# A retention layer with an ELU feed-forward: one early load asked for later, and an opening planned with other piece times

## The chip, the cores and the metric

The kernel runs on one core of one Trainium2 chip. The metric is the device time of one execution in microseconds, over several runs. The core has a matrix engine (TensorE, PE in the profile, with a separate path PEld that loads weights), a vector engine (VectorE, DVE), an engine for activations and copies (ScalarE, ACT), a general engine (GpSimd, POOL) and an engine that only issues transfers (SyncE, SP). Each engine works through its own list of instructions in order; between engines they wait on semaphores. Transfers can be asked for by SP, ACT and POOL; 16 DMA engines carry them out.

## What is computed

Retention over 8 batches, 8 heads, 576 positions and 64 values per head, then a feed-forward with 512 inputs, 2048 hidden values and an ELU:

```python
scores = scale * np.matmul(q, k.transpose(0, 1, 3, 2))
gamma = 1.0 - 2.0 ** (-5.0 - np.arange(H, dtype=np.float32))
Dmat = np.where(rel >= 0, gamma[:, None, None] ** rel[None, :, :], 0.0)
attn = np.matmul(scores * Dmat[None], v)             # q, k, v: (8, 8, 576, 64)
x = attn.transpose(0, 2, 1, 3).reshape(B * S, H * D)     # (4608, 512)
h = x @ w_in                                             # w_in: (512, 2048)
g = np.where(h > 0.0, h, np.exp(np.minimum(h, 0.0)) - 1.0)
out = g @ w_out                                          # w_out: (2048, 512)
```

## The kernel before

The 512 first positions of each batch are cut into 4 items (2 stretches of 256 positions, called T, by 2 groups of 4 heads, called w); the 64 last positions of all batches make two more items, the tails. An item n goes through these named steps:

- **ldq, ldk, ldv**: its 256 KB pieces of q, k and v are loaded by SP (L375). One of them, v of item 0, is loaded by ScalarE instead; the table `AWAY` (L203) names it and the earliest time at which the planner may place it.
- **cq, ck**: q and k times their decay factors (tiles gq, gk), in two halves each (`scaled`, L445); cq10 is half 1 of q of item 0. **cv**: v cast to bf16 (`cast_v`, L479). They run on DVE, POOL or ACT.
- **T, cp**: four transposes on PE and the copy of their result into tile qkT (`turn_pe`, L491 and L497); T(1,0) is q of item 1, T(1,1) its k.
- **sc, mask**: the products of q and k into tile sc, and their masking on DVE into tile pt (L731).
- **st, mid, end, bm, be**: the running state. st multiplies k by v on PE; mid and end add it up (L678, L680, L687), bm and be spread it into the tiles s_mid and s_end (L709, L695).
- **iv, xc**: on PE, state times queries plus pt times values (`do_inter`, `do_values`); the result is copied into tile xt (L766) by ACT or DVE.

The feed-forward then works on blocks. The first blocks have 256 positions, later ones 512. **F1** (`ffn1`) is 8 matmuls with w_in for a narrow block; **ex** is the exponential on ACT (L878), **md** either a relu (ACT L888 or DVE L890) or, later, an addition on DVE (L892), **g** the last step of the ELU on DVE (L900, L902). **F2** (`ffn2`) multiplies by w_out. The weights come in eight pieces **wi0..3** and **wo0..3**, asked for by POOL (L424, L432). Items 0 to 3, that is batch 0, feed blocks 0 and 1 (F1_0_p and F1_1_p).

The order of the steps on each engine is not written out. Every step is an `Op` with a cost in microseconds for each engine that may run it, the steps it depends on and a rank. `Plan.run` (L66) plays these through: when an engine is free it takes the ready step with the lowest rank; a step with several engines goes to the one that would end it first. Between a step's end and the start of a step on another engine the planner counts `HOP` (L19). The weight pieces have earliest times in `FROM` (L200). The program is then emitted in the planned order, and the chip keeps that order on every engine, but not the planned times. Where the plan leaves PE without work in the first 50 us, matmuls on a tile of zeros are put in its place.

A step `hold4` (L384) on POOL keeps SP's load of q of item 4, and so all of SP's later loads, back until POOL comes to it. The decay factors are three exponentials on ACT (L973 to L975, step `factors`). The completion of the transfers that SP and ACT ask for is counted on eight semaphores that the framework hands out in turn: a ninth transfer waits, before it is issued, until the first one on the same semaphore has landed.

Of the kernel before, what the change touches and what calls it, by code (L numbers as in the profile page):

```python
# [11 lines left out]
FP32 = mybir.dt.float32  # L12
BF16 = mybir.dt.bfloat16
I32 = mybir.dt.int32
AF = mybir.ActivationFunctionType
ALU = mybir.AluOpType

P = 128
HOP = {"PE": 0.22, "DVE": 0.08, "ACT": 0.08, "POOL": 0.1}  # L19
LANES = 6  # L20


class Op:


    def __init__(self, name, cost, deps, emit, rank, take=(), use=(), banks=(), dma=None, after=None):
        self.name, self.cost, self.emit, self.rank = name, cost, emit, rank
        self.deps = [d for d in deps if d is not None]
        self.turn = [] if after is None else [after]
        self.take, self.use, self.banks, self.dma = take, [*use, *(t[1] for t in take)], banks, dma  # L30
        self.eng = self.start = self.end = self.done = None
        self.slot, self.waits, self.at = {}, [], 0.0


class Plan:
# [6 lines left out]
    def add(self, *a, **kw):  # L42
        op = Op(*a, **kw)
        self.ops.append(op)
        for key in op.use:
            self.users.setdefault(key, []).append(op)
            op.turn += self.owner.get(key, [])
        for cls, key, *_ in op.take:
            self.owner[key] = [op]
            if cls not in FREE:  # L50
                op.turn += self.takers.get(cls, [])
                self.takers[cls] = [op]
        return op
# [12 lines left out]
    def run(self, began):  # L66

        self.left = {key: len(u) for key, u in self.users.items()}
        self.freed = {}
        bank, lanes = {}, {"SP": 0, "POOL": 0, "ACT": 0}  # L70
        wire = {"SP": [], "POOL": [], "ACT": []}
        free, order, events = dict(began), [], []
# [51 lines left out]
        while len(order) < len(self.ops) or any(wire.values()) or events:  # L124
            again = True
            while again:
                again = False
                for e in began:
                    if free[e] > now + 1e-9:
                        continue  # L130
                    best = pick(e, now)
                    if best is None:
                        continue
                    _, op, got = best
                    for o in op.cost:
                        ready[o].remove(op)
                    cost = op.cost[e]
                    op.eng, op.start, op.end = e, now, now + (cost[0] if isinstance(cost, tuple) else cost)
                    op.done = None
                    op.waits = [*op.deps, *(bank[b] for b in op.banks if b in bank and bank[b].eng != e)]  # L140
                    for b in op.banks:
                        bank[b] = op
                    op.slot = {}
                    for key, (cls, n) in got.items():
                        if self.slots[cls][n] is not None:
                            op.waits += self.users[self.slots[cls][n]]
                        self.slots[cls][n], op.slot[key] = key, n
# [40 lines left out]

LEAD = 64
HOLD = {4: "wi0"}  # L190
RANKS = {}
TOGETHER = 1
EARLY = 5
LOOSE = True
# [27 lines left out]
def kernel(  # L222
# [140 lines left out]
    def load_main(it, srcs="qkv"):  # L363
# [3 lines left out]
        for s in srcs:  # L367
# [14 lines left out]
            if s == "q" and n in HOLD:  # L382
                def emit_hold(op, key=key):
                    pin(nc.gpsimd.memset(tiles[key][:, 0, 0, :1], 0.0))  # L384

                held.append(add(f"hold{n}", {"POOL": 0.1}, [], emit_hold, -5, take=take))
# [33 lines left out]
    def load_w_in(n0, n1, after):  # L420
        c = slice(n0 * 512, n1 * 512)

        def emit(op):
            pin(nc.gpsimd.dma_start(w_in_sb[:, :, c], moe_w_in[:, c].rearrange("(j p) n -> p j n", p=P)))  # L424

        op = add(f"wi{n0}", {"POOL": 0.8}, [], emit, -1000, dma=(2.75 * (n1 - n0), 32 * (n1 - n0), 4.9), after=after)
        for n in range(n0, n1):
            w_in_ld[n] = op

    def load_w_out(n, after):  # L430
        def emit(op):
            pin(nc.gpsimd.dma_start(w_out_sb[:, 4 * n : 4 * n + 4],  # L432
                                    moe_w_out[n * 512 : (n + 1) * 512, :].rearrange("(f p) n -> p f n", p=P)))

        w_out_ld[n] = add(f"wo{n}", {"POOL": 0.8}, [], emit, -1000, dma=(2.75, 32, 4.9), after=after)

# [47 lines left out]
    def turn_pe(it, i, deps, src, key, dst_cls, n_of, cost):  # L484
# [3 lines left out]
        def emit(op):  # L488
            p = tiles["T", n_of]
            for j in range(4):  # L490
                pin(nc.tensor.transpose(p[:, j], src()[:, j * P : (j + 1) * P], ident))  # L491

        t = add(f"T{n_of}", {"PE": 0.35}, deps, emit, it.rank - 4,
                take=[T("f", ("T", n_of), [P, 4, P], BF16)])

        def emit2(op):
# [332 lines left out]

    def early(it):  # L830
        n = it.n
        sc = add(f"sc{n}", {"PE": 0.4}, it.turned, lambda op: do_scores(it), it.rank,
                 take=[T("sc", ("sc", n), [P, 2, 512], FP32)], use=[("qkT", n)])
# [3 lines left out]
        st = add(f"st{n}", {"PE": 0.3}, [it.cq[1, 0], it.cq[1, 1], it.cv], lambda op: do_state(it, views), it.rank + 1,  # L837
                 use=[("qkn", n), ("vn", n)])
        reserve(st, keys)
        after_state(it, st, views, [(keys[0], 0), (keys[1], 0)])  # L840
# [154 lines left out]
    for i, blk in enumerate(seq):  # L995
# [84 lines left out]
```

## Time and profile before

| | |
|---|---|
| runs | 306.06, 306.35, 307.82 us, median 306.35 |
| the profiled execution | 306.02 us; its span, first to last instruction: 303.8 us |
| PE busy | 294.5 us (97% of the span), 3281 matmuls seen |
| PEld, DVE, ACT, POOL busy | 171.0, 210.1, 158.6, 148.3 us |
| granted TensorE clock | 1.00 |
| read and written | 36.70 MB, 9.44 MB |

The costliest groups of instructions, by line, engine and operation, with busy time, mean time of one, and the idle time of the engine just before them:

```
L256 PE MATMUL f<-xt,w_in_sb 128*128 128x256 bf16 (+1 forms) x754 | 142.9, 325 | 1.0 <-DVE xt L766 0.3
L256 PE MATMUL f<-w_out_sb,g 128*128 128x512 bf16 (+2 forms) x580 | 139.8, 368 | 2.4 <-issue 1.3
L878 ACT ACTIVATE e<-f 128x512 f32<-128x512 f32 x144 | 85.6, 597 | 91.0 <-PE f L256 86.5
L892 DVE TENSOR_SCALAR em<-e 128x512 bf16<-128x512 f32 x90 | 44.5, 494 | 44.3 <-ACT e L878 43.8
L902 DVE SCALAR_TENSOR_TENSOR g<-f,em 128x512 bf16<-128x512 f32 x90 | 61.9, 689 | 7.1 <-DVE em L892 0.5
```

In a row of the timeline the columns are start, duration, engine, line, operation, tiles and shapes, count, and in brackets the engine's idle time before it with what ended it. "ACTq" and "SPq" are the queues in which an engine asks for transfers. Times in the text count from the start of the span.

### The profile page before, as it was taken

Reading aid. Unit: us, or ns where it says so; the run is one execution under the profiler, and the core shown is the slowest. Engines: PE = TensorE matmul, PEld = TensorE weight load, DVE = VectorE, ACT = ScalarE, POOL = GpSimd, SP = SyncE. Lnnn points to the kernel's source line nnn. Section 1 sums busy time; section 2 is a strip of 40 time slices with the busy share of each in tenths; the row PEclk is TensorE's granted clock in tenths of the full one; section 3 lists DMA queues with packets and bytes.
Section 4 is the critical chain, followed back from the end, with each engine's and each line's share of the span. In section 5 each row is a group of like instructions: output and inputs, shape, how many; then the busy total and the mean of one; then the engine's idle time right before and its main releaser. Section 6 shows DMA issues by size and latency. Waiting matters only on the chain.

```text
span 303.8 us, 8244 instructions
## 1 busy us (share of the span) xinstructions
PE 294.5 (97%) x3281; PEld 171.0 (56%) x3323; DVE 210.1 (69%) x380; ACT 158.6 (52%) x309; POOL 148.3 (49%) x252
## 2 busy tenths in 40 slices
PE   7899999999999999999999999999999999999996
PEld 3688656758767775554554444555554444444445
DVE  3978935749888888788787666768766666666600
ACT  4548724738765554687653434466544343444311
POOL 5980389987999998988886324322000000000000
PEclk9999999999999999999999999999999999999999
DMA  7999999999999999999997767311111111011132
GB/s 213 266 206 211 233 294 325 224 305 267 222 278 210 257 202 306 249 240 243 232 252 188 173 154 159 79 37 37 37 33 38 36 36 35 35 37 36 35 103 72
DMA packets 103991, 50.08 MB, mean 165 GB/s; under 512 B 45841, under 2 KB 99473, under 8 KB 103953
## 3 DMA queue, kind: packets, MB, share of 16 engines
q1 hardware_dynamic: 99200, 45.10, 67.4%
q0 software_dynamic: 4224, 4.19, 8.3%
q8 instruction: 26, 0.43, 0.6%
q10 hardware_dynamic: 528, 0.26, 0.3%
q14 instruction: 13, 0.10, 0.1%
HBM read 36.70 MB, written 9.44 MB: 152 GB/s over the span
## 4 chain that ended last, share of the span: by engine, by line
PE 92%; DVE 3%; DMA 2%; issue 1%; POOL 0%; SPq 0%; ACT 0%; POOLq 0%; ACTq 0%
PE f L256 88%; PE sc L256 4%; DMA rqk<-in_k_dram 2%; DVE qkn L445 1%; DVE pt L731 1%; PE f L491 1%; DVE g L900 0%; DVE f L890 0%; POOL qkn L445 0%; DVE qkT L497 0%; DVE s_mid L709 0%; SPq L375 0%; DVE xt L766 0%; DVE end L687 0%; DVE s_end L695 0%
## 5 line engine op out<-in xcount | busy, mean ns | idle before, releaser
L256 PE MATMUL f<-xt,w_in_sb 128*128 128x256 bf16 (+1 forms) x754 | 142.9, 325 | 1.0 <-DVE xt L766 0.3
L256 PE MATMUL f<-w_out_sb,g 128*128 128x512 bf16 (+2 forms) x580 | 139.8, 368 | 2.4 <-issue 1.3
L878 ACT ACTIVATE e<-f 128x512 f32<-128x512 f32 x144 | 85.6, 597 | 91.0 <-PE f L256 86.5
L256 PEld LDWEIGHTS <-w_in_sb 128*128 128x128 bf16 x768 | 73.3, 98 | 51.8 <-DVE xt L766 0.6
L256 PEld LDWEIGHTS <-g 128*128 128x128 bf16 x608 | 56.6, 98 | 58.9
L892 DVE TENSOR_SCALAR em<-e 128x512 bf16<-128x512 f32 x90 | 44.5, 494 | 44.3 <-ACT e L878 43.8
L902 DVE SCALAR_TENSOR_TENSOR g<-f,em 128x512 bf16<-128x512 f32 x90 | 61.9, 689 | 7.1 <-DVE em L892 0.5
L731 DVE TENSOR_TENSOR pt<-sc,mask 128x1024 bf16<-128x1024 f32 x32 | 38.9, 1215 | 5.3 <-PE sc L256 5.3
L445 POOL TENSOR_TENSOR qkn<-rqk,gq 128x256 bf16<-128x256 f32 x59 | 37.5, 648 | 10.2 <-DMA rqk<-in_q_dram 10.2
L900 DVE SCALAR_TENSOR_TENSOR g<-e,f 128x512 bf16<-128x512 f32 x54 | 36.4, 683 | 8.0 <-ACT f L888 7.6
L445 POOL TENSOR_TENSOR qkn<-rqk,gk 128x256 bf16<-128x256 f32 x62 | 38.6, 633 | 3.6 <-DMA rqk<-in_k_dram 3.6
L936 ACT COPY ot<-f 128x512 f32<-128x512 f32 (+2 forms) x36 | 20.2, 563 | 20.3 <-PE f L256 14.6
L766 ACT CAST xt<-f 128x256 bf16<-128x256 f32 x50 | 20.1, 450 | 18.6 <-PE f L256 18.5
L695 POOL TENSOR_TENSOR s_mid<-mid,diag 128x256 bf16<-128x256 f32 x29 | 17.8, 615 | 23.8 <-ACT mid L678 12.5
L888 ACT ACTIVATE f<-f 128x512 f32<-128x512 f32 x48 | 28.4, 595 | 0.0
L695 POOL TENSOR_TENSOR s_end<-end,diag 128x256 bf16<-128x256 f32 x31 | 19.6, 633 | 5.4 <-DVE end L687 5.3
L479 POOL CAST vn<-rv 128x512 bf16<-128x512 f32 x29 | 18.6, 643 | 2.4 <-DMA rv<-in_v_dram 2.4
L546 POOL TENSOR_TENSOR qkt<-rqt,gq 128x256 bf16<-128x256 f32 x16 | 10.5, 677 | 15.3 <-DMA rqt<-in_k_dram 15.3
L256 PE MATMUL sc<-qkT 64*64 64x128 bf16 x512 | 13.4, 222 | 0.0
L256 PE MATMUL f<-pt,vn 64*64 64x128 bf16 x512 | 12.7, 217 | 0.4 <-DVE pt L731 0.4
L256 PEld LDWEIGHTS <-qkT 64*64 64x64 bf16 x512 | 8.2, 106 | 4.0 <-DVE qkT L497 0.6
L687 DVE TENSOR_TENSOR end<-f,mid 128x128 f32<-128x128 f32 x32 | 9.0, 283 | 1.2 <-ACT mid L678 0.3
(69 smaller groups left out, 135.2 us busy)
## 6 DMA issues: line engine op xcount, KB each, us to landing
rqk<-in_q_dram SPq DMA_DIRECT2D x32, 256.0 KB, 5.3
rqk<-in_k_dram SPq DMA_DIRECT2D x32, 256.0 KB, 5.4
rv<-in_v_dram SPq DMA_DIRECT2D x31, 256.0 KB, 5.0
out_dram<-ot SPq DMA_DIRECT2D x26, 256.0 KB, 2.9
out_dram<-ot SPq DMA_DIRECT2D x19, 128.0 KB, 2.3
w_in_sb<-in_moe_w_in_dram POOLq DMA_DIRECT2D x4, 512.0 KB, 9.2
w_out_sb<-in_moe_w_out_dram POOLq DMA_DIRECT2D x4, 512.0 KB, 14.9
rqt<-in_q_dram SPq DMA_DIRECT2D x8, 128.0 KB, 3.2
```

The lines of the kernel that those rows point to most:

```text
L256: pin(nc.tensor.matmul(*a, **kw))
L445: pin(alu[op.eng].tensor_tensor(tiles[key][:, i, e], tiles[raw][:, :, e], g, ALU.mult))
L479: pin(copy[op.eng](tiles["vn", n], tiles["rv", n]))
L695: pin(alu[op.eng].tensor_tensor(tiles[key].rearrange("p h (j d) -> p h j d", j=2), tiles[src].unsqueeze(2).to_broadcast([P, 2, 2, D]), dia ...
L731: pin(nc.vector.tensor_tensor(tiles["pt", n].rearrange("p i h n -> p (i h) n"), tiles["sc", n].rearrange("p i (h n) -> p (i h) n", h=2), m ...
L766: pin(copy[op.eng](dst, src))
L878: pin(nc.scalar.activation(tiles[ekey], tiles[hkey], AF.Exp))
L888: pin(nc.scalar.activation(ph, ph, AF.Relu))
L892: pin(alu[op.eng].tensor_scalar_add(em, e, -1.0))
L900: pin(nc.vector.scalar_tensor_tensor(g, e, -1.0, ph, ALU.add, ALU.min))
L902: pin(nc.vector.scalar_tensor_tensor(g, ph, 0.0, tiles["em", blk, p], ALU.max, ALU.min))
L936: pin(copy[op.eng](tiles[okey][:, :cols], tiles[pkey][:, :cols]))
```

## The change

It has four parts. The planner's prices are set anew: a new table `LAP` takes 0.09 us (DVE), 0.11 us (ACT) or 0.03 us (POOL) off a step's time on its engine, `HOP` is 0.2, 0.135, 0.155 and 0.1 us, a table `BESIDE` adds time to a step of scaling or spreading that begins while the other of DVE and POOL runs such a step, and several costs are lowered. v of item 0 may not be placed before 3.45 us in place of 2.25 us, and ScalarE begins at 2.8 us in the plan, so that its load stands behind `factors`; a first activation on ScalarE, which used the tile of zeros, is gone. The weights get other earliest times. And a table `ON` fixes the engine of 13 steps of the opening, `RANKS` shifts the rank of five.

```diff
-HOP = {"PE": 0.22, "DVE": 0.08, "ACT": 0.08, "POOL": 0.1}
+LAP = {"PE": 0.0, "DVE": 0.09, "ACT": 0.11, "POOL": 0.03, "SP": 0.0}
+HOP = {"PE": 0.2, "DVE": 0.135, "ACT": 0.155, "POOL": 0.1}
+BESIDE = {"DVE": ("POOL", 0.4), "POOL": ("DVE", 0.2)}
...
-            if cls not in FREE:
+            if cls not in FREE and key not in LONE:
...
-                    op.eng, op.start, op.end = e, now, now + (cost[0] if isinstance(cost, tuple) else cost)
+                    pay = cost[0] if isinstance(cost, tuple) else cost
+                    if op.side and e in BESIDE and now + 0.15 < busy.get(BESIDE[e][0], 0.0):
+                        pay += BESIDE[e][1]
+                    if op.side:
+                        busy[e] = now + pay
+                    op.eng, op.start, op.end = e, now, now + pay - (LAP[e] if op.dma is None else 0.0)
...
-RANKS = {}
+RANKS = {"mid0": -14, "mid2": 3, "end3": 2, "be1": 6, "xc1_2": 11}
...
-FROM = (8.9, 9.7, 10.5, 13.3, 16.6, 17.4, 18.2, 19.6)
-ON = {}
+FROM = (7.6, 8.33, 9.87, 15.31, 16.14, 16.63, 17.85, 18.22)
+ON = {"ck01": "POOL", "ck02": "POOL", "ck12": "POOL", "cv0": "POOL", "be1": "POOL", "be2": "POOL", "be3": "POOL",
+      "cq11": "DVE", "be0": "DVE", "cp(3, 0)": "DVE", "xc0_2": "DVE", "xc1_2": "DVE", "md_1_2": "DVE"}
...
-AWAY = {("v", 0): 2.25}
+AWAY = {("v", 0): 3.45}
...
+LONE = (("rv", 0),)
...
-    first = const.tile([P, 1], FP32, name="first")
-    pin(nc.scalar.activation(first, zero[:, :1], AF.Exp))
...
+    for op in plan.ops:
+        op.side = len(op.cost) > 1 and op.name[:2] in ("cq", "ck", "ct", "cv", "bm", "be")
...
-    order = plan.run({"PE": 1.3, "DVE": 2.2, "ACT": 2.25, "POOL": POOL0, "SP": 0.8})
+    order = plan.run({"PE": 1.3, "DVE": 2.2, "ACT": 2.8, "POOL": POOL0, "SP": 0.8})
```

Costs: a weight piece 2.62 us of transfer in place of 2.75, T 0.3 in place of 0.35, sc of an early item 0.3 in place of 0.4, its st 0.25 in place of 0.3, hold 0.13 in place of 0.1. No tile's shape, no operation and no transfer's size changes.

What the new order looks like in the first 24 us, engine by engine (it follows from the built program, which holds for the order, not for times):

- ACT: factors, load of v of item 0, cp(1,0), cv1, xc0_0, xc1_0, cv2, mid1, ... Before: the load stood ahead of factors, and cp(0,0) and cv0 followed.
- POOL: cq10, mask_t, **cv0, wi0, wi1, ck01, wi2, ck02, ck12, cq03, cq13, ck13, bm2, be1, wi3, be2, wo0 to wo3, be3, hold4**. Before: cq10, mask_t, ck10, cq01, ck01, ck11, cv1, wi0 to wi2, cq12, ck02, be1, ck03, wi3, bm2, ck13, be2, wo0 to wo2, be3, wo3, hold4.
- DVE: cq00, ck00, ck10, cp(0,0), cq01, cp(0,1), cq11, mask0, ck11, **mid0**, bm0, end0, cq02, be0, cq12, cp(1,1), bm1, cp(2,0), mask1, cp(2,1), end1, ck03, mid2, mask2, cp(3,0), end2, mid3, bm3, end3, xc0_2, mask3, xc1_2.
- PE: T(0,0), T(0,1), sc0, T(1,0), 13 matmuls on zeros, **st0**, ..., iv2, sc3, F1_0_0, F1_0_1, iv3, F1_0_2, F1_0_3, F1_1_0. Before, the end of this was: st3, F1_0_0, sc3, F1_0_1, 7 matmuls on zeros, F1_0_2, iv3, F1_0_3, F1_1_0.
- In the program, the load of v of item 0 raises the semaphore that the load of k of item 0 raised, and carries a wait for it: it is issued when that k has landed. Before, it was among the first eight transfers and waited for nothing.

More of the change, by code (lines that the diff above doesn't have):

```diff
@@ L31, in __init__ @@
         self.eng = self.start = self.end = self.done = None
-        self.slot, self.waits, self.at = {}, [], 0.0
+        self.slot, self.waits, self.at, self.side = {}, [], 0.0, False
 class Plan:
@@ L69, in run @@
         self.freed = {}
+        busy = {}
         bank, lanes = {}, {"SP": 0, "POOL": 0, "ACT": 0}
@@ L384, in emit_hold @@
                     pin(nc.gpsimd.memset(tiles[key][:, 0, 0, :1], 0.0))
-                held.append(add(f"hold{n}", {"POOL": 0.1}, [], emit_hold, -5, take=take))
+                held.append(add(f"hold{n}", {"POOL": 0.13}, [], emit_hold, -5, take=take))
                 holds.append((held[0], HOLD[n]))
@@ L424, in emit @@
             pin(nc.gpsimd.dma_start(w_in_sb[:, :, c], moe_w_in[:, c].rearrange("(j p) n -> p j n", p=P)))
-        op = add(f"wi{n0}", {"POOL": 0.8}, [], emit, -1000, dma=(2.75 * (n1 - n0), 32 * (n1 - n0), 4.9), after=after)
+        op = add(f"wi{n0}", {"POOL": 0.8}, [], emit, -1000, dma=(2.62 * (n1 - n0), 32 * (n1 - n0), 4.9), after=after)
         for n in range(n0, n1):
@@ L433, in emit @@
                                     moe_w_out[n * 512 : (n + 1) * 512, :].rearrange("(f p) n -> p f n", p=P)))
-        w_out_ld[n] = add(f"wo{n}", {"POOL": 0.8}, [], emit, -1000, dma=(2.75, 32, 4.9), after=after)
+        w_out_ld[n] = add(f"wo{n}", {"POOL": 0.8}, [], emit, -1000, dma=(2.62, 32, 4.9), after=after)
     def scaled(it, i, e, cost):
@@ L491, in emit @@
                 pin(nc.tensor.transpose(p[:, j], src()[:, j * P : (j + 1) * P], ident))
-        t = add(f"T{n_of}", {"PE": 0.35}, deps, emit, it.rank - 4,
+        t = add(f"T{n_of}", {"PE": 0.3}, deps, emit, it.rank - 4,
                 take=[T("f", ("T", n_of), [P, 4, P], BF16)])
@@ L831, in early @@
         n = it.n
-        sc = add(f"sc{n}", {"PE": 0.4}, it.turned, lambda op: do_scores(it), it.rank,
+        sc = add(f"sc{n}", {"PE": 0.3}, it.turned, lambda op: do_scores(it), it.rank,
                  take=[T("sc", ("sc", n), [P, 2, 512], FP32)], use=[("qkT", n)])
@@ L836, in early @@
         views = [(keys[c], 0, lambda c=c: tiles[keys[c]][:, :P]) for c in range(2)]
-        st = add(f"st{n}", {"PE": 0.3}, [it.cq[1, 0], it.cq[1, 1], it.cv], lambda op: do_state(it, views), it.rank + 1,
+        st = add(f"st{n}", {"PE": 0.25}, [it.cq[1, 0], it.cq[1, 1], it.cv], lambda op: do_state(it, views), it.rank + 1,
                  use=[("qkn", n), ("vn", n)])
```

## The prediction

> **What bounds the kernel.** I read four views. First PE's waits from 24 us to 292 us (released engine and line, by whom: us in total, times, longest):
>
> ```profile
> PE f L256 <- issue: 1.3, 8, 0.2
> PE f L256 <- DVE xt L766: 0.3, 1, 0.3
> PE f L256 <- PE f L256: 0.2, 1, 0.2
> ```
>
> In 268 us PE waited once for another engine, 0.3 us, at 24 us. From there on it is full, so the change can win or lose only by the moment at which PE becomes full, or by holes that it opens later. So second the chain of work that ended last, at its start (start, us, what):
>
> ```profile
> 1.32 4.73 DMA rqk<-in_k_dram
> ```
>
> k of item 0 lands at 6.05 us, and the chain goes on over POOL and PE to DVE. Third DVE's rows of the timeline from there:
>
> ```profile
> 7.42 0.42 DVE L497 COPY qkT<-f 128x512 bf16<-128x512 bf16 x1 [0.85 <-PE f L491]
> 7.76 0.51 DVE L445 TENSOR_TENSOR qkn<-rqk,gq 128x256 bf16<-128x256 f32 x1
> 8.19 0.41 DVE L709 TENSOR_TENSOR s_mid<-f,diag 128x256 bf16<-128x256 f32 x1
> 8.52 1.21 DVE L731 TENSOR_TENSOR pt<-sc,mask 128x1024 bf16<-128x1024 f32 x1
> 9.65 0.27 DVE L687 TENSOR_TENSOR end<-f,mid 128x128 f32<-128x128 f32 x1
> 9.85 0.41 DVE L497 COPY qkT<-f 128x512 bf16<-128x512 bf16 x1
> 10.18 0.41 DVE L695 TENSOR_TENSOR s_end<-end,diag 128x256 bf16<-128x256 f32 x1
> 10.52 0.83 DVE L445 TENSOR_TENSOR qkn<-rqk,gq 128x256 bf16<-128x256 f32 x1
> 11.27 0.41 DVE L709 TENSOR_TENSOR s_mid<-f,diag 128x256 bf16<-128x256 f32 x1
> ...
> 12.93 0.41 DVE L445 TENSOR_TENSOR qkn<-rqk,gk 128x256 bf16<-128x256 f32 x1
> 13.27 1.58 DVE L445 TENSOR_TENSOR qkn<-rqk,gq 128x256 bf16<-128x256 f32 x2
> ```
>
> From 7.42 us DVE works without a hole until its third mask ends at 16.94. Two steps in a row start closer together than one lasts (7.42 to 7.76, 0.34 us, for a step of 0.42). A scaling step (L445) takes 0.41 to 0.51 us or, beside POOL, 0.79 to 0.83 us. Fourth the rows of ScalarE's load, of POOL's weight pieces, and of the point at which PE becomes full:
>
> ```profile
> 1.24 0.49 ACTq L375 DMA_DIRECT2D rv<-in_v_dram  x1
> ...
> 2.85 0.32 ACT L973 ACTIVATE gq<-expo,bq 128x32 f32<-128x32 f32 x1 [0.55 <-DVE expo L287]
> ...
> 9.95 2.41 POOL L424 DMA_DIRECT2D w_in_sb<-in_moe_w_in_dram  x3
> ...
> 22.16 1.26 PE L256 MATMUL f<-xt,w_in_sb 128*128 128x256 bf16 x10
> 23.74 0.50 PE L256 MATMUL f<-xt,w_in_sb 128*128 128x256 bf16 x3 [0.32 <-DVE xt L766]
> ```
>
> In the row at 22.16 the first 8 matmuls are F1_0_3 and two are F1_1_0's, whose third starts at 23.74. At 0.11 us each, F1_1_0 could have started at 23.52 without loss. In both orders the same work of PE lies ahead of F1_1_0, so this moment is what I compare.
>
> **The change part by part.** *The first activation on ScalarE goes*: 0.20 us at 2.10, but the factors wait for DVE's expo (0.55 us idle before 2.85), which nothing moves. Worth nothing; if that cover went, 0.2 us at most.
>
> *The load of v of item 0.* It leaves the start. q of item 0 landed 3.0 us after its issue at 0.81, thus at 3.8, and k of item 0 then follows it directly: 256 KB at some 290 GB/s (the stretches from 8 to 11 us) are 0.90 us, so k lands at 4.7; the other bound is 6.05 - 0.90 = 5.15. I take 4.7, since q's landing is a measured row. DVE may begin ck00 1.35 us earlier. But v is not asked for at 3.45 us: its load waits for that k, because it raises the same semaphore. It is issued at 4.75. From issue to landing its own row took 4.2 us beside SP's loads; q's 3.0 us in an empty queue is the bound below; one more SP load ahead of it (0.90) gives 5.1 above. I take 4.2, the same transfer beside the same company: v lands at 8.95, 3.5 us later than before (1.24 + 4.2 = 5.44).
>
> Of the transfer's sharing the Trainium skill says (DMA: Bandwidth & Descriptors, Queues, rings and completion order) that each DMA engine goes round the queues that have work, packet by packet. By an estimate from that rule v would get half of the 290 GB/s, 1.8 us, and with the 2.1 us that q's 3.0 us leave beside its own 0.90 it would land 3.9 us after its issue; the total would be 0.3 us lower. The row above, 4.2 us, roughly agrees.
>
> *What stands behind v.* On POOL cv0 (0.62 us, by the row of the same cast at 9.40) is now third; wi0, wi1, ck01 and everything after are queued behind it. In POOL's rows before, wi0 was asked for at 9.95; now at 8.95 + 0.05 + 0.62 = 9.6, so the weights keep their time. On PE st0 stands behind cv0, and on DVE mid0 behind st0. DVE has cq00 to ck11 done by about 8.8 and then sits idle: mid0 starts at 4.7 + 0.05 + 4.2 + 0.05 + 0.62 + 0.05 + 0.32 (16 matmuls of st) + 0.05 = 10.04.
>
> *DVE from there to cp(3,0)*, start to start from the rows: mid or end 0.20 (four: mid0, end0, end1, mid2), bm 0.33 (two), cp 0.34 (three), mask 1.13 (two), the last copy 0.42 to its end: 0.80 + 0.66 + 1.02 + 2.26 + 0.42 = 5.16 us. Four more, cq02, be0, cq12 and ck03, scale or spread beside POOL: 0.34 us each alone, 0.75 beside it. The six such rows between 7.76 and 14.77 stand at 0.43, 0.34, 0.75, 0.34, 0.75, 0.75, mean 0.56: 2.24 us (1.36 to 3.0). Sum 7.40; cp(3,0) ends at 17.44. POOL's ck12 is through by 13.8 (9.6 + two weight pieces 1.6 + ck01 0.6 + wi2 0.8 + two steps 1.2), so T(2,1) is not late for cp(2,1); DVE is the chain.
>
> *PE from there*: four matmuls on zeros that wait for that copy's bank 0.27, iv2 0.66 (16.77 to 17.43), sc3 0.35, F1_0_0 and F1_0_1 1.76 (0.88 each, 20.61 to 21.49) with 0.2 for a wait for xc0_2, iv3 0.67, F1_0_2 and F1_0_3 1.76, and a wait in F1_0_3 for ScalarE's two copies of item 3: they start 1.0 us after iv3 ends, as at 23.24 before, take 0.77, and the fourth matmul would be 1.2 us behind iv3: 0.6 us. Sum 6.3: F1_1_0 starts at 23.75, against 23.52. The 7 matmuls on zeros that went (0.4 us) are in it.
>
> *The overlap that the plan now counts on.* The rows say 0.34 for 0.42, and the sum uses the 0.34. [...]
>
> *Later stretches.* The new prices move some 17 of md from ScalarE's relu to DVE's addition: 17 x 0.49 = 8 us more on DVE, which was busy 69%. No wait of PE of before shows it, so I take nothing; if that cover goes, it is the last rival. Next late is item 4: hold4 comes after wo3 and be3 on POOL, at about 22.25 by the same count of steps (before 21.44), so q of item 4 lands 0.8 us later than before (30.12) and POOL's two steps (1.18) end at 32.15. PE comes to that transpose at 32.27 + 0.23. It just fits.
>
> **Sum.** The profiled execution took 306.02 us, 2.2 more than its span, 0.33 under the median. 23.75 - 23.52 = 0.23 on 306.35: about **306.6**.
>
> **Rivals.** *The opening gets shorter.* If v landed by 7.7 us, 3.0 us after its issue like q, mid0 would start at 8.8, where DVE is free, 1.24 us earlier: 306.6 - 1.24 = 305.35; with all four scalings at 0.34, 0.9 less, 304.5. For it: k lands earlier, DVE starts earlier; against it: v's own 4.2 us. The turning point between gain and loss is a landing at 8.7.
>
> *v lands a load later* (5.1 us after its issue). POOL's list slides by 0.9 us, mid0 with it, and hold4 passes 23: q, k and v of item 4 then come after PE is ready for them. 306.6 + 0.9 = 307.5, with the scalings at 0.75 another 0.4 or so. Slower than before, from a landing at 8.7 on. For it: SP's loads took 5 to 6 us in that stretch; against it: they queue behind each other.
>
> *PE's clock.* PE would idle 1.6 us before st0 (T(1,0) and its zeros end at about 8). At the start, from 1.26 to about 4.65 us, the weight loads between the 128x512 zeros stand 0.43 us apart; later eight matmuls of that size take 1.90 us (at 41.06), 0.22 each. Back at the slow pace for as long as that, 3.4 us, PE would lose 1.7 us: 308.3. The Trainium skill (TensorE: Matmul & The Clock Gate, Part 1) puts the fall-back behind about 3.4 us of idleness, which would not be reached; the longest hole of the rows, 0.7 us, shows no fall.
>
> *A plan without slack.* With its margins counted off, DVE comes late for g in many places of 40 to 200 us: PE's waits would grow past 3 us, 309.5 or more. For it: 8 us more on DVE; against it: 268 us with 0.3 us of waiting.
>
> *The load would not move at all*: excluded, it stands behind factors in ScalarE's list, and its wait holds it further.
>
> **Numbers.** Chances: forecast (306.0 to 307.1) 0.50; shorter opening 0.22, of which 0.02 below 303.3; v a load later 0.18; clock 0.04; no slack 0.06. Range 304.9 to 307.9: it takes in both first rivals and leaves out 0.1 above and some 0.04 below. About 1%, 3.1 us, is what I count as told from no change: faster 0.02, same 0.92, slower 0.06.
>
> **What would show it.** ACTq's load at 4.8 us and v landing at 8.95; cv0 on POOL at 9.0; a hole of DVE of about 1.2 us before mid0 at 10.0; cp(3,0) ending at 17.4; F1_1_0 at 23.75; hold4 at 22.25; PE's waits from 24 us on as small as before. It is wrong if v lands before 8 us or after 9.6, or if PE waits for DVE, POOL or a load after 24 us.

## The result, and the profile after

| | before | after |
|---|---|---|
| median | 307.17 us (306.06 to 307.82, 6 runs) | 311.08 us (310.16 to 312.32, 6 runs) |
| ratio of the times | | 1.0134, 95% interval 1.0101 to 1.0168 |
| the same in a second job | 306.24 us (17 runs) | 310.14 us (6 runs), 1.0136 (1.0114 to 1.0158) |
| the profiled execution | 306.02 us, span 303.8 | 312.32 us, span 310.6 |
| granted TensorE clock | 1.00 | 0.994 |

The changed kernel is 1.3% slower; 306.6 with a range to 307.9 was forecast. The profiled execution of the changed kernel is the slowest of its first six and that of the kernel before the fastest: the two profiles lie 6.3 us apart, the medians 3.9, so the lines below show up to 2.4 us more of a loss than the medians have. A ratio leaves out executions more than 1.5% above the fastest of their kernel; in the runs below this concerns e13 alone, two of whose six are left out of its 1.0119.

PE's waits from 24 us to 292 us (by whom: us in total, times, longest):

```profile
PE f L266 <- issue: 1.9, 12, 0.2
PE f L266 <- ACT xt L774: 0.5, 1, 0.5
PE f L266 <- DVE xt L774: 0.3, 1, 0.3
PE f L266 <- PE f L266: 0.3, 2, 0.2
PE f L499 <- POOL qkn L453: 0.3, 1, 0.3
```

PE is still full: 1.1 us of waiting for other engines, 0.8 of it before 29 us. The loss lies ahead of that. The chain of work that ended last, three of its pieces (start, us, what):

```profile
1.32 3.37 DMA rqk<-in_k_dram
4.71 5.95 DMA rv<-in_v_dram
...
27.46 13.12 DMA rqk<-in_k_dram
```

k of item 0 lands at 4.69, 1.36 us earlier than before, and its place in the chain is taken by v of item 0: asked for at 4.71, landed at 10.66. The third piece is k of item 4, asked for late and landed at 40.58. What stood behind v, on the other engines' rows of the timeline:

```profile
4.71 0.43 ACTq L383 DMA_DIRECT2D rv<-in_v_dram  x1
...
10.79 0.61 POOL L487 CAST vn<-rv 128x512 bf16<-128x512 f32 x1 [5.42 <-DMA rv<-in_v_dram]
11.35 1.68 POOL L432 DMA_DIRECT2D w_in_sb<-in_moe_w_in_dram  x2
...
21.42 0.80 POOL L432 DMA_DIRECT2D w_in_sb<-in_moe_w_in_dram  x1
...
26.83 0.13 POOL L392 MEMSET rqk<- 128x1 f32 x1
...
28.37 9.44 PE L266 MATMUL f<-xt,w_in_sb 128*128 128x256 bf16 x85 [0.51 <-ACT xt L774]
```

POOL stands idle for 5.42 us; cv0 and its whole list slide. The row at 26.83 is hold4 (21.44 before). 27 matmuls of F1 lie ahead of the row at 28.37, so F1_1_0 starts five matmuls of 0.11 us into it: 28.92, against 23.52 before. DVE's rows between mid0 and cp(3,0):

```profile
11.81 0.29 DVE L686 COPY mid<-f 128x128 f32<-128x128 f32 x1 [2.03 <-PE f L266]
...
12.54 0.42 DVE L453 TENSOR_TENSOR qkn<-rqk,gq 128x256 bf16<-128x256 f32 x1
12.87 1.41 DVE L703 TENSOR_TENSOR s_end<-end,diag 128x256 bf16<-128x256 f32 x1
14.21 2.26 DVE L453 TENSOR_TENSOR qkn<-rqk,gq 128x256 bf16<-128x256 f32 x1
16.39 0.41 DVE L505 COPY qkT<-f 128x512 bf16<-128x512 bf16 x1
...
19.06 0.42 DVE L505 COPY qkT<-f 128x512 bf16<-128x512 bf16 x1 [0.38 <-PE f L499]
...
20.85 1.23 DVE L739 TENSOR_TENSOR pt<-sc,mask 128x1024 bf16<-128x1024 f32 x1 [0.63 <-PE sc L266]
21.99 0.42 DVE L505 COPY qkT<-f 128x512 bf16<-128x512 bf16 x1
```

The last row is cp(3,0). Two steps beside POOL, be0 at 12.87 and cq12 at 14.21, hold DVE for 1.34 and 2.18 us (to the start of the next), where 0.34 is the price alone; and from 18 us on DVE waits for PE twice, 1.01 us. PE is slow there. The table by stretches (stretch, its length, then busy time and count of PE, PEld, DVE, ACT, POOL, the granted clock, DMA share, GB/s):

```profile
16.00:17.00 1.00, 0.47 (x13) 0.31 (x16) 1.00 (x3) 0.00 (x0) 1.00 (x3) 1.00 1.24 204
17.00:18.00 1.00, 1.00 (x23) 0.83 (x17) 1.00 (x3) 0.27 (x1) 0.51 (x1) 0.50 1.24 207
18.00:19.00 1.00, 1.00 (x14) 0.80 (x16) 0.69 (x1) 0.00 (x0) 0.00 (x0) 0.50 1.25 208
19.00:20.00 1.00, 1.00 (x26) 0.74 (x29) 0.94 (x4) 0.00 (x0) 0.00 (x0) 0.50 1.24 205
20.00:21.00 1.00, 1.00 (x38) 0.91 (x38) 0.37 (x3) 0.39 (x2) 0.70 (x2) 0.80 1.24 208
```

The clock is 0.50 from 17 us to about 20.4 (0.80 in the last stretch is 0.4 us at half). PE had idled 2.30 us from 9.15 (for cv0) and 1.94 us from 14.59 (for cq12).

### The profile page after: what moved, and what is told of

The parts are those of the page before. It is cut to its first block, busy times and chain, and to the rows that moved or that the text cites. A ratio compares the mean times of both kernels' runs of the same rounds, so it can differ in the third digit from the quotient of the medians.

```text
span 310.6 us, 8224 instructions
## 1 busy us (share of the span) xinstructions
PE 296.5 (95%) x3269; PEld 172.4 (56%) x3310; DVE 219.4 (71%) x397; ACT 150.2 (48%) x293; POOL 147.9 (48%) x250
## 4 chain that ended last, share of the span: by engine, by line
PE 86%; DMA 7%; DVE 3%; issue 1%; POOL 1%; SPq 0%; ACT 0%; ACTq 0%; POOLq 0%
PE f L266 82%; DMA rqk<-in_k_dram 5%; PE sc L266 4%; DMA rv<-in_v_dram 2%; DVE qkn L453 1%; PE f L499 1%; DVE s_end L703 0%; DVE pt L739 0%; POOL qkn L453 0%; PE f L1051 0%; DVE xt L774 0%; DVE s_mid L703 0%; DVE g L908 0%; DVE end L695 0%; POOL vn L487 0%
## 5 line engine op out<-in xcount | busy, mean ns | idle before, releaser
L900 DVE TENSOR_SCALAR em<-e 128x512 bf16<-128x512 f32 x107 | 53.2, 498 | 46.3 <-ACT e L886 46.1
L910 DVE SCALAR_TENSOR_TENSOR g<-f,em 128x512 bf16<-128x512 f32 x107 | 73.6, 689 | 7.9 <-DVE em L900 0.5
L453 POOL TENSOR_TENSOR qkn<-rqk,gq 128x256 bf16<-128x256 f32 x59 | 38.6, 666 | 11.3 <-DMA rqk<-in_q_dram 11.3
L453 POOL TENSOR_TENSOR qkn<-rqk,gk 128x256 bf16<-128x256 f32 x60 | 37.5, 642 | 2.4 <-DMA rqk<-in_k_dram 2.4
L944 ACT COPY ot<-f 128x512 f32<-128x512 f32 (+2 forms) x38 | 21.3, 564 | 22.4 <-PE f L266 19.4
L908 DVE SCALAR_TENSOR_TENSOR g<-e,f 128x512 bf16<-128x512 f32 x37 | 24.7, 681 | 2.9 <-ACT f L896 2.3
L896 ACT ACTIVATE f<-f 128x512 f32<-128x512 f32 x31 | 18.5, 596 | 0.0
L554 POOL TENSOR_TENSOR qkt<-rqt,gq 128x256 bf16<-128x256 f32 x16 | 10.1, 651 | 16.2 <-DMA rqt<-in_k_dram 16.2
L266 PE MATMUL f<-vn,qkn 64*64 64x64 bf16 x512 | 9.6, 194 | 2.4 <-POOL vn L487 2.3
## 6 DMA issues: line engine op xcount, KB each, us to landing
w_out_sb<-in_moe_w_out_dram POOLq DMA_DIRECT2D x4, 512.0 KB, 12.2
```

The source lines that it names most:

```text
L266: pin(nc.tensor.matmul(*a, **kw))
L453: pin(alu[op.eng].tensor_tensor(tiles[key][:, i, e], tiles[raw][:, :, e], g, ALU.mult))
L896: pin(nc.scalar.activation(ph, ph, AF.Relu))
L900: pin(alu[op.eng].tensor_scalar_add(em, e, -1.0))
L908: pin(nc.vector.scalar_tensor_tensor(g, e, -1.0, ph, ALU.add, ALU.min))
L910: pin(nc.vector.scalar_tensor_tensor(g, ph, 0.0, tiles["em", blk, p], ALU.max, ALU.min))
```

## The experiments

My theory after the result: the load's wait for k makes v land late, and everything else follows from that. Rivals: the falling clock, DVE's steps beside POOL, POOL's list and its weights, and the rest of the new plan. All runs in one table. Its first four columns of numbers come from the profiled execution of each run, its last two from all executions; the profiled one of the changed kernel is slower than its median, so a difference in F1_1_0 need not be one of the medians. "v" is v of item 0; "wi0" and "F1_1_0" are the times at which that weight piece is asked for and that step starts, without a stall inside it.

| run | v lands | wi0 | v of item 3 lands | F1_1_0 | median us | ratio to before |
|---|---|---|---|---|---|---|
| before | 5.4 | 9.9 | 14.8 | 23.5 | 306.2 to 307.2 | |
| after | 10.7 | 11.3 | 14.1 | 28.9 | 311.08 | 1.0134 |
| e1_load_first | 5.0 | 6.8 | 21.8 | 30.6 | 313.18 | 1.0230 (1.0213 to 1.0247) |
| e2_no_wait | 8.4 | 9.1 | 15.4 | 24.2 | 307.28 | 1.0032 (1.0006 to 1.0058) |
| e3_before_behind | 11.0 | 8.8 | 14.2 | 27.3 | 309.96 | 1.0123 (1.0105 to 1.0140) |
| e4_warm | 10.3 | 11.0 | 14.8 | 27.8 | 311.01 | 1.0158 (1.0132 to 1.0184) |
| e5_weights_in_gap | 11.5 | 12.2 | 14.8 | 27.6 | 310.47 | 1.0148 (1.0128 to 1.0168) |
| e7_rest_alone | 5.2 | 8.1 | 17.9 | 27.2 | 308.51 | 1.0066 (1.0043 to 1.0089) |
| e8_weights_later | 5.0 | 11.0 | 13.9 | 24.2 | 306.73 | 1.0019 (1.0009 to 1.0029) |
| e9_third_later | 6.7 | 11.9 | 15.3 | 25.5 | 308.21 | 1.0068 (1.0055 to 1.0081) |
| e10_hold_sp | 9.6 | 10.3 | 14.3 | 26.9 | 310.09 | 1.0125 (1.0108 to 1.0141) |
| e11_cq12_first | 10.6 | 11.3 | 14.3 | 26.7 | 310.82 | 1.0151 (1.0128 to 1.0174) |
| e12_copy_dve | 5.0 | 11.1 | 13.9 | 24.0 | 306.59 | 1.0016 (1.0005 to 1.0027) |
| e13_v_fifth | 8.0 | 8.7 | 22.0 | 30.7 | 311.13 | 1.0119 (1.0084 to 1.0154) |
| e14_fifth_later | 8.7 | 12.3 | 15.9 | 24.5 | 308.75 | 1.0071 (1.0044 to 1.0098) |
| e15_both | 10.4 | 11.0 | 15.5 | 26.0 | 308.97 | 1.0097 (1.0080 to 1.0114) |

The kernel before ran beside each job (medians 306.2 to 306.3 there).

**The wait taken away.** The load is put into the program among the first eight transfers, behind factors, so that it waits for nothing; SP's load of q of item 2 is held by a copy of a decay factor:

```diff
+        pin(nc.vector.tensor_copy(tiles["rqq", 2][:, 0, 0, :1], gk[:, 0, :1]))
+        load_q2(op)
...
+    order.remove(by["factors"])
+    order.remove(by["ldv0"])
+    order[:0] = [by["factors"], by["ldv0"]]
```

> The changed kernel's order, with v of item 0 behind the factors on ScalarE but with no wait for k of item 0 (SP's load of q of item 2 waits instead for a copy of one factor, about 3.7 us, so that v's load is the sixth transfer). Theory A1 (transfers land in the order in which they were asked for, over both queues, some 0.9 us apart): v is asked for at about 3.4 and lands sixth, at about 8.9 us; time 307.2 to 308.2. Rival A2 (ScalarE's queue takes its half of the DMA engines at once): v lands 4.2 us after it was asked for, at about 7.6; time 306 to 307. If the wait for k is not what matters, the time stays at the changed kernel's 311.

The load's issue, the cast and PE's longest wait in the opening, by the timeline:

```profile
2.86 0.50 ACTq L383 DMA_DIRECT2D rv<-in_v_dram  x1
...
7.87 0.42 PE L266 MATMUL sc<-qkT 64*64 64x128 bf16 x16 [0.87 <-DVE qkT L505]
...
8.50 0.61 POOL L487 CAST vn<-rv 128x512 bf16<-128x512 f32 x1 [3.36 <-DMA rv<-in_v_dram]
```

Asked for 1.85 us earlier, v lands 2.3 us earlier, PE has no hole over 0.87 us, and the time is 307.28: some three quarters of the loss is gone (1.0134 to 1.0032). The load is asked for at 2.86, ahead of v of item 1, so it lands fifth and not sixth, at 8.4, between the two expectations (8.9 and 7.6); the time is in the range of the first. The load stands behind factors here too (it is issued while the first of them runs), so its place in ScalarE's list is harmless; what costs is the wait.

**The load's move alone**, in the order of the kernel before:

```diff
+    order.remove(by["ldv0"])
+    order.insert(order.index(by["factors"]) + 1, by["ldv0"])
```

> The order of the kernel before on every engine, with only the load of v of item 0 moved behind the factors; it again carries the wait for k of item 0. Theory A: v lands at about 10.7 us as in the changed kernel and the time rises by 3 to 5 us, to 310 to 312. Theory B (the new order is what costs): the time rises by less than 1 us.

Its issue, and PE's first work with it:

```profile
5.17 0.44 ACTq L375 DMA_DIRECT2D rv<-in_v_dram  x1
...
11.68 0.32 PE L256 MATMUL f<-vn,qkn 64*64 64x64 bf16 x16 [4.22 <-ACT vn L479]
```

It lands at 11.0, and the ratio is 1.0123: nine tenths of what the whole change costs.

**The clock.** More matmuls on zeros ahead of st0 (38) and ahead of item 2's first transposes (20), so that PE stays busy while it waits:

```diff
-            if gap > 0:
+            if gap > 0 or op.name == "T(2, 0)":
...
-                for n in range(int(gap * 0.8 / 0.056)):
+                for n in range(int(gap * 0.8 / 0.056) + {"st0b0": 38, "T(2, 0)": 20}.get(op.name, 0)):
```

> The changed kernel with 38 more matmuls on zeros before st0 and 20 before the transposes of q of item 2, where PE stood idle 2.30 and 1.94 us. Theory C (PE's idleness drops the granted clock to 0.50 for 3.4 us, from 17.0 to 20.4 us, and this is part of the price): the clock stays at 1.00 and the time falls by 0.7 to 1.7 us, to 309.4 to 310.4. If the slow stretch lies beside DVE's chain anyway, the clock stays at 1.00 and the time does not move by more than 0.4 us.

Two of the stretches shown above, in this run:

```profile
17.00:18.00 1.00, 1.00 (x31) 0.86 (x29) 1.00 (x2) 0.04 (x1) 0.12 (x1) 1.00 1.20 201
18.00:19.00 1.00, 1.00 (x42) 0.80 (x39) 1.00 (x5) 0.21 (x1) 0.00 (x0) 1.00 1.27 210
```

The clock stays at 1.00, and the median does not move: 311.01. Taken by itself this says that the fall costs nothing; cq12 still takes 2.26 us here.

**The load first**, all else as changed:

```diff
+    order.remove(by["ldv0"])
+    order.insert(0, by["ldv0"])
```

> The changed kernel's order on every engine, with one difference: ScalarE asks for v of item 0 as its first instruction, ahead of the factors. Theory A (the load's late landing, 10.66 us in the changed kernel's trace, is what costs the time: POOL, PE and DVE stand behind it): v lands second, at about 5.4 us, k of item 0 at about 6.0, the first weight piece is asked for before 10.5, PE's holes before 17 us stay under 1 us each and the granted clock stays at 1.00; time within 0.7 us of the kernel before (about 307.2). Theory B (the new order is bad by itself, DVE being starved beside POOL's steps that follow each other): the time stays 2 us or more above the kernel before, 309 or more.

The first expectation failed: v lands at 5.0, and the time is 313.18, worse than with the wait. It lies in the range of the second, but not by its cause: be0 and cq12 take 0.83 and 0.41 us here. Three rows tell why, POOL's first weight pieces, ScalarE's cast of v of item 3, and PE behind it:

```profile
6.81 1.68 POOL L432 DMA_DIRECT2D w_in_sb<-in_moe_w_in_dram  x2
...
21.88 0.62 ACT L487 CAST vn<-rv 128x512 bf16<-128x512 f32 x1 [5.97 <-DMA rv<-in_v_dram]
22.55 0.43 PE L266 MATMUL f<-vn,qkn 64*64 64x64 bf16 x16 [2.79 <-ACT vn L487]
```

With POOL no longer held by v, the weights are asked for at 6.81 and their transfers run while item 3's loads are on the way: its v lands 13.2 us after it was asked for at 8.63. This is a second fault of the change, which the first one hides.

**The rest of the change alone** (v first as before, `first` restored, the plan made anew) and **the weights later**:

```diff
-AWAY = {("v", 0): 3.45}
+AWAY = {("v", 0): 2.25}
...
```

> The rest of the change alone: v of item 0 is loaded first on ACT as before, the first activation stands again, and the plan is made anew with the new prices and piece times. Theory A (the piece times 7.6, 8.33, 9.87 ask for the weights too early as soon as POOL isn't held by v): wi0 and wi1 are asked for at about 8, their packets take half of the DMA engines while item 3's loads are on the way, v of item 3 lands after 18 us (14.8 before), PE gets holes of over 2 us between 15 and 23 us, and the time is 309.5 to 313. Theory B (the rest of the change is harmless, and all of the loss is the load's wait for k): 305.3 to 307.3, like the kernel before, with v of item 3 by 15.5 us.

```diff
+    order.insert(0, by["ldv0"])
+    order.remove(by["wi0"])
+    order.insert(order.index(by["ck02"]) + 1, by["wi0"])
...
+    order.insert(order.index(by["ck12"]) + 1, by["wi2"])
```

> The changed order with v of item 0 first on ACT (as in the run with the load first, 313.18) and with wi0 and wi1 asked for behind ck02 and wi2 behind ck12 on POOL. Theory A (in the run with the load first the weights came in the way of item 3's loads): wi0 is asked for at about 10.1, v of item 3 lands by 16 us instead of 21.85, PE's clock stays at 1.0, and the time falls from 313.2 to 305 to 307.3. Theory B (the order of the changed plan is slow for another reason, such as DVE's two-input steps beside POOL's): it stays above 309.5.

The rest alone lies between its two expectations: wi0 is asked for at 8.1, v of item 3 lands at 17.9, PE waits 1.71 and 1.95 us, 1.0066. In e8 the first weight pieces and the load of v of item 3 (KB, us to landing) are these:

```profile
11.01 1.68 POOL L432 DMA_DIRECT2D w_in_sb<-in_moe_w_in_dram  x2
...
rv<-in_v_dram SPq DMA_DIRECT2D x1, 256.0 KB, 5.2
```

With only the weights moved, e8 takes 306.73 where e1 took 313.18; v of item 3 needs 5.2 us instead of 13.2. So the weights were e1's loss, shown by moving nothing else. What is left of the whole change is then 0.2%.

**POOL's list.** In the changed kernel, three weight pieces go into the 2.8 us in which POOL waits for mid2:

```diff
+    order.remove(by["wi3"])
+    order.insert(order.index(by["bm2"]), by["wi3"])
...
```

> The changed kernel with three weight pieces (wi3, wo0, wo1) asked for ahead of bm2 on POOL, in the 2.8 us in which POOL waits for mid2, instead of behind be1. Theory A (what late v costs runs through POOL's list: wi3 is asked for at 21.4 us and lands at 27.4, so F1_0_3 and then item 4's loads are late): wi3 is asked for at about 17.5 and lands at about 24.8, the stretch in which PE becomes full moves ahead by some 2.5 us, and the time falls from 311.1 to 308 to 309.3. Theory B (what late v costs runs through DVE alone, mid0 to cp(3,0), and the weights are hidden behind it): the time stays at 310.4 to 311.6 although wi3 lands earlier.

wi3 is asked for 3 us earlier, hold4 comes at 24.80, and the median is 310.47 beside 311.08 and 310.14 of the changed kernel in two jobs: no difference. The weights and item 4's loads are not what most of the loss is made of.

**DVE beside POOL.** ck02 on POOL waits for cq12:

```diff
...
+        pin(nc.gpsimd.tensor_copy(spare, tiles["qkn", 2][:, 0, 1, 0, :1]))
+        step(op)
...
```

> The changed kernel with one edit on POOL: ck02 waits for DVE's cq12 (a one-element copy from cq12's result ahead of it), so that POOL's four scaling steps in a row no longer run beside cq12. Theory A (DVE's steps starved beside POOL are on the path that sets the end): cq12 takes 0.5 us or less instead of 2.26, cp(3,0) ends 8.4 to 9.4 us behind the start of mid0 instead of 10.6, and the time is 0.8 to 1.8 us under that of the changed kernel in the same job. Theory B (what DVE gains, POOL's later ck12 and cq13 give back): DVE waits for PE ahead of cp(2,1) instead, and the time is within 0.5 us of the changed kernel's.

be0, cq12 and the copy behind it:

```profile
12.81 0.42 DVE L704 TENSOR_TENSOR s_end<-end,diag 128x256 bf16<-128x256 f32 x1
13.14 0.83 DVE L454 TENSOR_TENSOR qkn<-rqk,gq 128x256 bf16<-128x256 f32 x1
15.06 0.42 DVE L506 COPY qkT<-f 128x512 bf16<-128x512 bf16 x1 [1.08 <-PE f L500]
```

cq12 falls from 2.26 to 0.83 us, but then DVE waits 1.08 us for PE's transposes: PE's clock is at 0.50 from 12 to 15 us in this run. The median, 310.82 beside 310.14 for the changed kernel in the same job (`after_again`), is no better, which is the second expectation, though the wait is not where it was expected (ahead of cp(1,1), not of cp(2,1)).

> The changed kernel as it is, for comparison on the same chip with the two edits of it in this job. All theories expect 310.2 to 311.5 beside 306.3 for the kernel before, a ratio of 1.013 to 1.017, and v of item 0 landing 5.5 to 7 us after its issue at 4.7.

**Both together.** Neither edit alone moved the time, and in each the other's trouble stood behind it. The last run has both, the wait of ck02 and the 38 matmuls on zeros ahead of st0:

```diff
+        pin(nc.gpsimd.tensor_copy(spare, tiles["qkn", 2][:, 0, 1, 0, :1]))
...
+                for n in range(int(gap * 0.8 / 0.056) + {"st0b0": 38}.get(op.name, 0)):
```

> The changed kernel with ck02 on POOL behind cq12 and with 38 more matmuls on zeros ahead of st0, so that neither the clock falls nor cq12 is starved. Each edit alone left the time where it was: without the fall cq12 still took 2.26 us; with cq12 at 0.83 us PE, at half speed from 12 to 15 us, let DVE wait 1.08 us ahead of cp(1,1). Theory A (each hid the other): the clock stays at 1.0, DVE waits under 0.4 us ahead of cp(1,1), mid0 to the end of cp(3,0) takes 7.2 to 7.8 us, F1_1_0 starts by 26.0 with v at 10.3 to 10.7, and the ratio to the kernel before is 1.007 to 1.011. Theory B (v's landing alone sets the time, by hold4 and the loads behind it): the ratio stays at 1.013 to 1.016.

be0, cq12, the copy behind it, and cp(3,0):

```profile
12.84 0.83 DVE L704 TENSOR_TENSOR s_end<-end,diag 128x256 bf16<-128x256 f32 x1
13.60 0.41 DVE L454 TENSOR_TENSOR qkn<-rqk,gq 128x256 bf16<-128x256 f32 x1
13.93 0.41 DVE L506 COPY qkT<-f 128x512 bf16<-128x512 bf16 x1
...
18.73 0.41 DVE L506 COPY qkT<-f 128x512 bf16<-128x512 bf16 x1
```

None of these takes over 0.83 us, and DVE waits for nothing between them. v lands at 10.4, as late as ever, F1_1_0 starts at 25.95, and the ratio falls from 1.0136 to 1.0097 (1.0080 to 1.0114), as the first expectation had it. This interval lies below those of e4 and e11 and touches that of `after_again` at 1.0114: some 1.2 us of the loss was these two, each hidden by the other. The rest, 1%, is left with a v of 10.4.

**What is ahead of v.** The wait for k is kept (by a one-element copy from that k), and SP's loads from v of item 1 on are held as well, in e10 behind cq10, in e13 behind mask_t on POOL; e14 is e13 with the weights later:

```diff
+        pin(nc.gpsimd.memset(tiles["rv", 1][:, 0, 0, :1], 0.0))
+        load_v1(op)
...
+        pin(nc.scalar.copy(tiles["rv", 0][:, 0, 0, :1], tiles["rqk", 0][:, 0, 0, :1]))
+        load_v0(op)
```

> The changed kernel, v of item 0 still asked for on ACT only when k of item 0 has landed (a one-element copy from that k into v's tile holds it), but SP's loads from v of item 1 on are held too, by a one-element write on POOL behind cq10, so that only q and k of item 1 are ahead of v when it is asked for at about 5.0. Theory A (v lands late because SP's loads asked for earlier are served first): v lands by 8.4, 3.4 us or less after its issue, st0 starts by 9.2, and the time is 306.8 to 308.3. Theory B (a load on ACT's queue beside SP's takes 5.5 us or more whatever was asked for before): v lands at 10.5 or later and the time stays at 310.3 to 311.7.

> As the run that held SP's loads, but with the one-element write on POOL behind mask_t, so that v of item 1 and all after it are asked for on SP at about 5.45, behind v of item 0 (asked for at 5.0 on ACT, still only when k of item 0 has landed). Only q and k of item 1 are then ahead of it. Theory A (loads land in the order in which they were asked for, over both queues, 0.9 us each and not under 3.0 us): v of item 0 lands fifth, at 8.0 to 8.6, ahead of v of item 1; mid0 starts by 10.0; PE's longest hole is under 1.5 us, its clock stays at 1.0, and the time is 306.8 to 308.0 although the wait for k is still there. Theory B (the wait for k costs its time whatever is ahead in the queues): v lands at 9.5 or later and the time is 309.5 to 311.

> The run before (v of item 0 behind the wait for k, but fifth in the order of asking; it landed at 7.97, and then k and v of item 3, asked for around the weights, landed at 18.36 and 21.99) with wi0 and wi1 asked for behind ck02 and wi2 behind ck12, as in the run with v first and the weights later. Theory A (two causes and no third: the loads ahead of v, and the weights ahead of item 3's loads): v of item 0 lands by 8.6, wi0 is asked for at 11 or later, v of item 3 lands by 15.5, PE's clock stays at 1.0, and the time is 306.6 to 307.8, with the wait for k still in the kernel. Theory B (the wait, or what else the change holds, costs time by another way): 309 or more.

In e10 SP was released at 4.68, ahead of ACT's 5.01: v of item 1 stayed in front, and v landed sixth, at 9.6, between the two expectations, with no gain in time. In e13 the load is fifth, and lands 3.0 us after its issue. Four transfers of e13 (KB, us to landing), from a profile of an execution of 313.1 us, where its six took 308.1 to 313.8:

```profile
rv<-in_v_dram ACTq DMA_DIRECT2D x1, 256.0 KB, 3.0
rv<-in_v_dram SPq DMA_DIRECT2D x1, 256.0 KB, 3.3
...
rqk<-in_k_dram SPq DMA_DIRECT2D x1, 256.0 KB, 10.2
rv<-in_v_dram SPq DMA_DIRECT2D x1, 256.0 KB, 12.3
```

v at 7.97, mid0 at 9.54, no hole of PE until 15 us: as the first expectation had it, with the wait still there. Then the weights, asked for at 8.66, come in the way of k and v of item 3 (the two last lines), and the time is lost again. e14 removes that too: F1_1_0 starts at 24.5 and the clock stays at 1.00, as expected, but the time is 308.75, 1 us above the expected. Its profile has 1.6 us of PE's waiting that no other run has:

```profile
PE sc L266 <- DMA qkT<-qkn: 1.6, 3, 0.8
```

These waits are for transposing transfers, two of the three between 100 and 125 us. Why they come late there I did not test, so what is left of the loss in e14 stays open.

**v third on SP** and **a copy on DVE.** e9 asks for v on SP behind k and sets the weights later in the plan; e12 is e8 with xc0_3 on DVE.

> v of item 0 is no load of ScalarE at all but the third load on SP behind k, with the weights' times 2.3 to 1.6 us later (9.9, 10.7, 11.5, 14.3, then as before), and the plan made anew. Theory A (what counts is that v lands by about 7 us and the weights leave item 3's loads alone): v of item 0 lands at about 5.6, q of item 1 at 6.5, v of item 3 by 15.5, wi0 is asked for at about 10.3, PE's clock stays at 1.0, and the time is 304.8 to 306.8. Theory B (the new plan with its overlapping steps loses by itself): 308.5 or more, with waits of PE for DVE or POOL after 24 us.

> The run with v first and the weights later (306.73) with one copy of item 3's output (xc0_3) moved from ACT to DVE ahead of md_0_1, beside the other copy on ACT. Theory A (the 0.51 us that PE waits in F1_0_3 for ACT's second copy is on the path): the wait shrinks to 0.15 us or less and the time is 306.1 to 306.5, level with the kernel before. Theory B (md_0_1 and g_0_1 behind it on DVE become late instead): PE waits for g later and the time stays at 306.6 to 307.

e9 lands v at 6.7, and every load of item 1 one place later; with F1_1_0 at 25.5 it takes 308.21, between its expectations, and PE waits for nothing after 24 us. e12 takes the wait from 0.51 to 0.21 us and gives 306.59 for 306.73, about the second expectation. No version was faster than the kernel before.

## Why the prediction was wrong

**What failed: the landing of v.** "From issue to landing its own row took 4.2 us beside SP's loads ... v lands at 8.95", with 5.1 as the upper bound. It took 5.95 us. The row of before is that of a load with one load ahead of it. At 4.71 us five were ahead. The transfers asked for from 4 to 5 us in the changed kernel (KB, us to landing):

```profile
rqk<-in_k_dram SPq DMA_DIRECT2D x1, 256.0 KB, 5.9
rv<-in_v_dram ACTq DMA_DIRECT2D x1, 256.0 KB, 6.0
rv<-in_v_dram SPq DMA_DIRECT2D x1, 256.0 KB, 6.7
```

k of item 2, asked for at 4.10, lands at 10.0; v of item 0, asked for at 4.71, at 10.7; v of item 2, asked for at 4.93, at 11.6. They land in the order of asking over both queues, and so they do in before (q, v, k of item 0), e2, e10 and e13. In the second profile of the changed kernel, e4, e11 and e15, v came in 0.2 to 0.9 us ahead of k of item 2, which was asked for 0.4 to 0.6 us before it but took 1.0 to 1.7 us to issue. Counted in the order of asking, q and k of item 1, v of item 1, q and k of item 2 and v itself are 6 x 0.90 = 5.4 us behind k's 4.69: 10.1, for 10.66 measured. The rows of before held all of this. I had the same rule in "one more SP load ahead" and added one load where there were more. The Trainium skill (DMA: Bandwidth & Descriptors, Queues, rings and completion order) has each DMA engine go round its queues packet by packet; the 3.9 us I worked out from it is further from 5.95 than my own 4.2, so here the trace does not bear out an equal share for the queue with one load.

**What followed from it, term by term** (profiled execution, to F1_1_0; 28.92 - 23.75 = 5.17 us too late):

- mid0 1.77 late (11.81 for 10.04), the landing's 1.71 and 0.06.
- The four steps beside POOL took 4.18 us (0.33, 1.34, 2.18, 0.33) for 2.24, above the bound of 3.0: 1.94. The mean was taken over steps that last 0.75 us at most beside POOL; here POOL ran four steps in a row beside cq12.
- DVE's waits for PE at the slow clock, a term that the sum put at nothing: 1.01. The rest of that stretch: 0.25. Without these two the term was right: from mid0 to the end of cp(3,0) e15 needs 7.37 us (11.77 to 19.14) and e2 7.53 (9.89 to 17.42), for 7.40 forecast.
- PE from cp(3,0) to F1_1_0: 6.51 for 6.3, 0.2.

**F1_1_0 as the measure** was right. The span less its start is 280.3 us before, and 280.7 in e2, e4, e5, e8 and e13, though that start differs by 6.5 us among them. In the changed kernel's profile it is 281.7, and where the 1.0 on top comes from is open. "hold4 at 22.25" was 26.83 there, k of item 4 landed at 40.58, and T(4,0) waited 0.28 us for POOL; but e13, with hold4 at 25.33, has 280.7, and e15, with hold4 at 23.84, has 281.2.

**The rivals.** "v a load later" was the right one by its mechanism, mis-sized in the landing (5.1 us), and it priced 0.9 us of landing at 0.9 to 1.3 of time. In the runs 2.3 us of landing (e2 to after) go with 4.7 us of F1_1_0 and with 1% of the time, 3.1 us, and the steps beside POOL and the clock, 1.2 us of the time in e15, go with it. Its price for a hold4 past 23 did not show: with hold4 at 24.8 and 25.4, in e5 and e4, PE waited for no load of item 4. Its turning point between gain and loss, a landing at 8.7, is not borne out: with v at 8.4, e2 is still 0.3% slower than before (1.0006 to 1.0058). "PE's clock" (0.04) came, with less idleness than I asked for; its price, 1.7 us by my sum, shows only where DVE is not starved at the same time, and both together are 1.2 us. "A plan without slack" did not come: after 30 us PE waits for DVE nowhere, although DVE is busy 9.3 us longer (219.4).

**What held:** k at 4.69 (4.7), the issue at 4.71 (4.75), the first activation's place in the cover of expo, steps of 0.33 to 0.34 us from start to start in the new order too (12.54 to 12.87), 17 md on DVE for nothing, wi0's landing (17.0 for 17.1 before). The Trainium skill (VectorE: DVE Perf Modes, The DRAIN you can't avoid) has the next step of DVE start when the pipe is empty, and adds that a step which is not held starts earlier. The trace, with 0.33 us from start to start for steps of 0.42, shows the earlier start.

**What I did not see at all:** that the weights' new times were safe only because v held POOL. The prediction found that "the weights keep their time" and asked no further; for its rival with v early it promised 305.35, and e1, with v at 5.0, took 313.18. Two causes are shown, then: v's late landing, by e2 and e3 (and that it comes from the loads ahead of it, by e13's opening), and the weights that come in the way of item 3's loads as soon as v is early, by e8.

## What to carry to other kernels

The time from issue to landing belongs to the place in line, not to the transfer: to price a load that is asked for later, count the loads asked for ahead of it on every queue that are not yet through. When a wait holds back an engine that also issues other transfers, ask what the wait protects, and try its removal with those transfers held as well. And where two delays run side by side, an experiment that removes one and finds nothing has not shown that it is free: remove both.

## What the runs showed of the hardware

- **The clock falls after less idleness than a whole window.** It fell to 0.50 in nine profiles, for 3.4 us or twice or three times that (6.8 in e1 and e13, 10.2 in the second profile of the changed kernel). In the 3.4 us ahead of each of these falls PE had been idle for 1.76 (e1) to 3.09 us (e5) in sum; in the eight profiles without a fall, for at most 1.53 us in any 3.4 us of the opening. One hole alone does not decide it. In e1 the fall came at 19.80, 0.04 us into the longest hole, after two of 1.25 and 1.37; in the changed kernel no fall followed the hole of 2.30 us at 9.15, and one came at 16.99, behind the hole of 1.94 that began at 14.59. The Trainium skill (TensorE: Matmul & The Clock Gate, Part 1) speaks of a free-running window of 3413 ns and an idle window of that length. The length of the falls agrees, and so may the free running: counted back from the fall at 16.99 in steps of 3.41, two windows would meet at 10.17, inside the hole of 2.30. That a whole window must be idle is not borne out.
- **DVE next to POOL.** A scaling step of 128x256 took 0.42 us alone, 0.83 beside one step of POOL and 2.26 beside four in a row, in four profiles alike (2.26, 2.26, 2.27, 2.27); with POOL's four behind it, the same step took 0.83 in e11 and 0.41 in e15. The Trainium skill (GPSIMD Engine Reference, 1. Specifications) names contention for steps of DVE with two inputs in SBUF; no size is given there.
- **Weights against loads.** In the three runs in which POOL asked for wi0 at 6.8, 8.1 and 8.7 us, v of item 3 landed at 21.8, 17.9 and 22.0; in all others, with wi0 at 8.8 or later, by 15.9. In those three, wi0 was asked for 0.25 to 1.8 us ahead of that load.
